# One constant filling product behind each of the first four left-half products of the second layer's tail

## The chip, the cores and the metric

The kernel runs on one core of a Trainium2 chip. The metric is the device time of one execution in microseconds (us); lower is better. Before the change three runs took 203.88, 204.24 and 204.27 us, a median of 204.24 us.

## The reference

Attention over 32 pooled memory slots feeds a soft mixture of eight experts. Per batch and head (8 batches, 8 heads, 576 tokens, 64 wide), and then over all 4608 tokens of 512 numbers:

```
a = softmax(phi, over tokens)                    # 576 x 32
k_m, v_m = a.T @ k, a.T @ v
attn = softmax(q @ k_m.T / 8) @ v_m              # x: 4608 x 512 over all heads
logits = x @ moe_phi                             # 4608 x 32 slots
slot_input = softmax(logits, over tokens).T @ x  # 32 x 512, four slots an expert
h = relu(slot_input[e] @ w1[e])                  # 512 -> 1024, 8 experts
slot_out[e] = h @ w2[e]                          # 1024 -> 512
out = softmax(logits, over slots) @ slot_out     # 4608 x 512
```

All inputs and the output are float32. The weights w1 and w2 are 16.8 MB each and the output is 9.4 MB.

## The kernel before

The work is a list of operations, each with an engine, an estimated cost, the tiles it reads and writes, and a priority. `Plan.order` simulates the engines with these costs and fixes one order per engine; the chip then runs each engine's list in that order, with waits on semaphores. All transfers to and from memory are issued by SyncE (SP) on one hardware queue.

The attention of four pairs of batches takes the first 140 us or so. While it ends, the expert weights stream in. The first layer (`expert_in`, L1383) makes h for two groups of four experts. The second layer (`expert_out`, with `mult`, L1432) sums h @ w2 over 16 pieces of w2, one half of the 512 columns into one accumulator each: the left half (d=0) into `kvbank[:, 0]`, the right half (d=1) into `scbank`. Each piece and half is four matmuls of 128 rows by 32 columns, side by side in the array, over 256 moving columns.

The last NT=5 of the 16 pieces are the tail. `tail_out` loads them by halves of 512 KB: first the five left halves, then the five right halves. `tail_mult(0, n)` adds the five left products as their data lands. Then `slot_sums(0)` copies the left accumulator to `cS` (DVE, L1347), sums its four parts with one product with `rep` (PE, L1355), and splits the result into a high and a low part, `sr` (ACT, L1362; DVE, L1367). Two `direct` products (PE, L1571) give the first output tiles from `cS` itself, and `out_mult` (PE, L1587) gives all others from `sr` and the slot weights `cT`. The table `RIGHT` puts the five right-half products `tail_mult(1, m)` between the first left-half output tiles; behind the last of them `slot_sums(1)` does the same for the right columns. Every output tile is copied out of PSUM by ACT (L1563) or DVE (L1564) in turn, over four PSUM banks, and stored by SP (L1600): six stores of 128 KB, ten of 384 KB, then 768, 1536 and 2304 KB.

`fill(n, pri, r)` puts n products of the constant `ones` (128x128) with itself, 256 moving columns wide, into a part of PSUM that nothing reads (`kvbank[:, 1, 256:512]`, PE, L520). Until now the calls give it priorities of `FILL` and above, which the planner places where PE would otherwise wait. With `pri=None` the operation gets the next priority of its phase, like any other.

Of the kernel before, what the change touches and what calls it, by code (L numbers as in the profile page):

```python
# [20 lines left out]
class Plan:  # L21
# [24 lines left out]
    def add(self, eng, cost, fn, r=(), w=(), also=(), pri=None, dma=0.0, slack=0.0, after=()):  # L46
        cost, ni = cost if isinstance(cost, tuple) else (cost, 4)
        i = len(self.ops)
        deps = set()
        tiles = {}  # L50
        for x in r:
            for key in x:
                tiles[key[0]] = None
                if key in self.last_w:
                    deps.add(self.last_w[key])
        for x in w:
            for key in x:
                tiles[key[0]] = None
                if key in self.last_w:
                    deps.add(self.last_w[key])  # L60
                deps.update(self.reads.get(key, ()))
        for x in w:
            for key in x:
                self.last_w[key] = i
                self.reads[key] = []
        for x in r:
            for key in x:
                self.reads.setdefault(key, []).append(i)
        deps.discard(i)
        deps.update(after)  # L70
        tiles = [t for t in tiles if t.pool is not None]
        for t in tiles:
            t.users += 1
        need = tiles + [t for t in also if t not in tiles]
        if pri is None:
            pri = self.phase[0]
            self.phase[0] += self.phase[1]
        self.ops.append((eng, cost, fn, deps, pri, dma, tiles, need, slack, ni))
        return i
# [191 lines left out]
def kernel(  # L271
# [244 lines left out]
    def fill(n, pri, r=()):  # L516
        for _ in range(n):
            add(
                PE, WC,
                lambda: nc.tensor.matmul(  # L520
                    warm.ap, ones, ones.unsqueeze(1).to_broadcast([P, 2, P]),
                    start=True, stop=True,
                ),
                r=[ones_b, *r], w=[warm], pri=pri,
            )
# [799 lines left out]
    NT, NA = 5, 6  # L1325
# [11 lines left out]
    pacc = [b_kv.tile(), b_s2.tile()]  # L1337
# [87 lines left out]
    def mult(dst, e, i, t, d):  # L1425
        u = 2 * e + i
        wide = t.ap.rearrange("p (j t d) -> p j t d", j=2, t=2)
        for k in range(2):
            for j in range(2):

                x = 2 * k + j
                nc.tensor.matmul(  # L1432
                    dst[NS * x: NS * x + NS, :HD],
                    hT()[:, 4 * k + 2 * i + j, NS * e: NS * e + NS],
                    wide[:, j, k, d * HD: d * HD + HD],
                    start=(u == 0),
                    stop=(u == 2 * E - 1),
                    tile_position=(0, NS * x),
                )
# [29 lines left out]
    def tail_mult(d, n, after=()):  # L1469
        e, i, t = tails[n]  # L1470
        return add(
            PE, (0.45, 16), lambda: mult(pacc[d].ap[:, 0], e, i, t, d),
            r=[hTb.part(e // EG), t.part(d)], w=[pacc[d]], after=after,
        )
# [75 lines left out]
    tail_out()  # L1550
    for n in range(NT):
        tail_mult(0, n)
    for bp in range(1, NBP):
        plan.at(SLOT_AT[bp - 1])
        slots(bp)
# [131 lines left out]
```

## Time and profile before

| | |
|---|---|
| median of three runs | 204.24 us (203.88 to 204.27) |
| the profiled execution, its own time | 204.05 us |
| its span, first to last instruction | 202.3 us |
| PE busy | 169.4 us (84%) |
| DVE, POOL, ACT busy | 141.2 (70%), 95.7 (47%), 74.5 us (37%) |
| moved by DMA | 76.47 MB, mean 378 GB/s |
| mean granted TensorE clock | 0.946 of full speed |

The span is what the rows below are measured in; 1.75 us of the execution lie around it. A granted clock of 1.00 is 2.4 GHz and one of 0.50 is 1.2 GHz. A matmul of the program on float32 data shows as two records in the trace (x8 for the four matmuls of one `mult`).

### The profile page before, as it was taken

What the parts mean: (1) busy time and instruction counts of PE and PEld (TensorE: products, weight loads), DVE (VectorE), ACT (ScalarE), POOL (GpSimd) and SP (SyncE); (2) the same over time, 40 slices, a digit from 0 to 9 for tenths busy, and PEclk for the clock granted to TensorE, in tenths of its full rate; (3) what the DMA queues carried; (4) which work ended last, traced back from release to release, by engine and by line L of the source; (5) the groups of instructions that cost most, each with busy time, mean ns of one, the idle gap of its engine ahead of it and who ended that gap; (6) DMA issues with size and microseconds to landing.
All of it is one profiled execution on the core that took longest, in us unless ns stands there. A gap on an engine that the chain in (4) does not pass through costs nothing.

```text
span 202.3 us, 6086 instructions
## 1 busy us (share of the span) xinstructions
PE 169.4 (84%) x2607; PEld 109.0 (54%) x2607; DVE 141.2 (70%) x267; ACT 74.5 (37%) x191; POOL 95.7 (47%) x92
## 2 busy tenths in 40 slices
PE   7999638978599899797999789899999967999900
PEld 6777534645457387464675347565655624457500
DVE  6822641898986899999899996478999601458810
ACT  2022414555431755607463252110238301246600
POOL 7199204789891894889954275000036930000000
PEclk9999999999859999999999999999999995899975
DMA  6999999999999999999999999999999999589996
GB/s 201 366 392 394 381 387 385 386 388 379 402 381 391 386 383 395 387 395 398 421 399 399 421 421 423 416 423 420 416 418 416 352 348 334 202 287 322 402 416 292
DMA packets 31914, 76.47 MB, mean 378 GB/s; under 512 B 1936, under 2 KB 15760, under 8 KB 28176
## 3 DMA queue, kind: packets, MB, share of 16 engines
q1 hardware_dynamic: 31888, 76.09, 99.6%
q8 instruction: 20, 0.33, 0.7%
q14 instruction: 6, 0.05, 0.1%
HBM read 66.65 MB, written 9.44 MB: 376 GB/s over the span
## 4 chain that ended last, share of the span: by engine, by line
PE 43%; DMA 17%; DVE 12%; POOL 11%; SPq 6%; issue 4%; ACT 2%; DVEq 0%; POOLq 0%
DMA arena<-in_v_dram 9%; PE bank L1383 7%; PE bank L1587 6%; SPq L502 6%; PE scbank L813 5%; DMA arena<-in_moe_w_dram 5%; PE kvbank L704 5%; DMA arena<-in_phi_dram 4%; PE bank L882 4%; POOL arena L871 3%; POOL arena L669 3%; POOL arena L648 3%; PE bank L1010 2%; POOL arena L848 2%; DVE arena L606 2%
## 5 line engine op out<-in xcount | busy, mean ns | idle before, releaser
L648 POOL TENSOR_TENSOR arena<-arena 128x1152 f32<-128x1152 f32 x8 | 21.0, 2634 | 19.2 <-ACT arena L641 16.5
L591 DVE STREAM_TRANSPOSE arena<-top 128x1152 f32<-128x1152 f32 x16 | 21.6, 1354 | 8.2 <-DMA top<-in_q_dram 8.2
L704 PE MATMUL kvbank<-arena 64*32 64x128 f32 x1152 | 21.2, 279 | 6.6 <-ACT arena L657 2.5
L520 PE MATMUL kvbank<-ones 128*128 128x256 f32 x82 | 24.2, 434 | 2.4 <-ACT arena L728 1.3
L669 POOL TENSOR_TENSOR arena<-arena 128x128 f32<-128x128 f32 (+2 forms) x32 | 23.4, 731 | 3.2 <-ACT arena L657 1.3
L813 PE MATMUL scbank<-arena 64*64 64x288 f32 x256 | 22.9, 433 | 2.3 <-DVE arena L827 2.3
L1525 POOL TENSOR_TENSOR cT<-cS,cT 32x640 fp32r<-32x640 f32 (+1 forms) x8 | 11.4, 1420 | 26.2 <-ACT cT L1520 25.7
L871 POOL TENSOR_TENSOR arena<-arena,ssm 128x576 f32<-128x576 f32 x16 | 18.3, 1154 | 9.7 <-DVE ssm L867 7.9
L704 PEld LDWEIGHTS kvbank<-arena 64*32 64x32 f32 x1152 | 16.5, 107 | 11.3 <-issue 4.8
L848 POOL TENSOR_TENSOR arena<-arena,smx 128x576 f32<-128x576 f32 x16 | 18.4, 1154 | 6.5 <-DVE smx L843 6.5
L606 DVE TENSOR_REDUCE arena<-arena 128x128 f32<-128x1152 f32 x8 | 17.1, 2146 | 6.0 <-DMA arena<-in_phi_dram 5.9
L882 PE MATMUL bank<-arena 128*128 128x288 f32 x64 | 18.7, 425 | 1.3 <-DVE arena L874 0.8
L520 PEld LDWEIGHTS kvbank<-ones 128*128 128x128 f32 x82 | 16.3, 214 | 6.3 <-ACT arena L728 1.7
L1564 DVE COPY arena<-bank 128x256 f32<-128x256 f32 (+1 forms) x30 | 14.4, 510 | 6.4 <-PE bank L1587 5.0
L1587 PE MATMUL bank<-sr,cT 64*128 64x256 f32 (+1 forms) x100 | 15.2, 363 | 0.5 <-ACT arena L1563 0.2
L827 DVE STREAM_TRANSPOSE arena<-scbank 128x576 f32<-128x576 f32 x16 | 12.3, 766 | 4.4 <-PE scbank L813 4.3
L813 PEld LDWEIGHTS scbank<-arena 64*64 64x64 f32 x256 | 9.6, 137 | 9.9 <-DVE arena L827 3.7
L882 PEld LDWEIGHTS bank<-arena 128*128 128x128 f32 x64 | 11.2, 189 | 6.4 <-issue 1.7
L853 ACT ACTIVATE arena<-arena 128x576 f32<-128x576 f32 x16 | 10.9, 684 | 9.8 <-POOL arena L848 9.7
L1563 ACT COPY arena<-bank 128x256 f32<-128x256 f32 (+1 forms) x24 | 10.4, 445 | 9.8 <-PE bank L1587 8.4
L1587 PEld LDWEIGHTS bank<-sr,cT 64*128 64x128 f32 x100 | 10.1, 191 | 6.9 <-DVE arena L1564 4.1
L1383 PE MATMUL bank<-arena,SIM 128*32 128x256 f32 x224 | 13.2, 390 | 0.2 <-DVE SIM L1264 0.2
(135 smaller groups left out, 265.0 us busy)
## 6 DMA issues: line engine op xcount, KB each, us to landing
arena<-in_moe_w_dram SPq DMA_DIRECT2D x25, 1024.0 KB, 13.3
top<-in_q_dram SPq DMA_DIRECT2D x8, 1152.0 KB, 13.1
arena<-in_k_dram SPq DMA_DIRECT2D x8, 1152.0 KB, 10.1
arena<-in_v_dram SPq DMA_DIRECT2D x8, 1152.0 KB, 12.5
arena<-in_moe_w_dram SPq DMA_DIRECT2D x10, 512.0 KB, 9.2
arena<-in_phi_dram SPq DMA_DIRECT2D x8, 576.0 KB, 7.5
out_dram<-arena SPq DMA_DIRECT2D x10, 384.0 KB, 3.9
out_dram<-arena SPq DMA_DIRECT2D x1, 2304.0 KB, 7.9
```

Source lines behind the costliest of these rows:

```text
L520: lambda: nc.tensor.matmul(warm.ap, ones, ones.unsqueeze(1).to_broadcast([P, 2, P]), start=True, stop=True,),
L591: lambda: nc.vector.transpose(qT.ap.rearrange("p (i u y) -> p u i y", i=2, y=Y), qt.ap[:, h * QT_SZ: h * QT_SZ + QT_SZ].rearrange("p (u i ...
L606: lambda: nc.vector.tensor_reduce(mx.ap[:, c0:c1], ph().rearrange("p c j m -> p c m j"), axis=AX.X, op=ALU.max),
L648: lambda: nc.gpsimd.tensor_tensor(ph(), ph(), mb.ap[:, c0:c1].unsqueeze(2).to_broadcast([P, c1 - c0, J, M]), op=ALU.subtract,),
L669: plus = lambda o, x, y: nc.gpsimd.tensor_tensor(o, x, y, op=ALU.add)
L704: nc.tensor.matmul(acc.ap[M * c: M * c + M, a, : 2 * D], ph()[h0: h0 + HALF, c, j, :], kv()[h0: h0 + HALF, :, c, j * D: j * D + D], start= ...
L813: nc.tensor.matmul(scb.ap[HALF * g: HALF * g + HALF, a, :JY], pair[g].kd.ap[h0: h0 + HALF, i, c].rearrange("p r m -> p (r m)"), pair[g].qT ...
L848: lambda: nc.gpsimd.tensor_tensor(exv(), exv(), bc(mx), op=ALU.subtract),
L871: lambda: nc.gpsimd.tensor_tensor(exv(), exv(), bc(sm), op=ALU.mult),
L882: nc.tensor.matmul(lp.ap[:, :JY], vpb.ap[:, h, :], aT.ap[:, a * JY: (a + 1) * JY], start=(h == 0), stop=(h == H - 1),)
L1383: nc.tensor.matmul(hb.ap[NS * j: NS * j + NS, :256], SIM.ap[:, 2 * i + c, NS * e: NS * e + NS], wv[:, c, 512 * (j // 2): 512 * (j // 2) + ...
L1587: nc.tensor.matmul(po.ap[:, : x.stop - x.start], cT[bp].ap[y: y + HALF, j // 2 * P: j // 2 * P + P], sr.ap[y: y + HALF, t, x], start=(t == 0),
```

## The change

Behind each of the first four left-half products of the tail, one filling product is put on the list, as a reader of the left accumulator, so that the planner places it after that product and before the next one.

```
     for n in range(NT):
         tail_mult(0, n)
+        if n < NT - 1:
+            fill(1, None, [pacc[0]])
     for bp in range(1, NBP):
```

On PE, before, the right product of the piece ahead of the tail and then the five left products of the tail, up to the sum of `slot_sums(0)`. `DMAHW` names the transfer a product waits for:

```order
L1432 MATMUL scbank<-arena 32x256 x4
L1432 MATMUL kvbank<-arena 32x256 [waits DMAHW4_49]
L1432 MATMUL kvbank<-arena 32x256 x3
L1432 MATMUL kvbank<-arena 32x256 [waits DMAHW5_49]
L1432 MATMUL kvbank<-arena 32x256 x3
L1432 MATMUL kvbank<-arena 32x256 [waits DMAHW6_49]
L1432 MATMUL kvbank<-arena 32x256 x3
L1432 MATMUL kvbank<-arena 32x256 [waits DMAHW7_49]
L1432 MATMUL kvbank<-arena 32x256 x3
L1432 MATMUL kvbank<-arena 32x256 [waits DMAHW0_49]
L1432 MATMUL kvbank<-arena 32x256 x3
L1355 MATMUL bank_65<-cS,rep 128x256 [waits DVE_49]
```

And now, on PE, from the end of the first of these left products to the end of the fifth:

```order
L520 MATMUL kvbank<-ones 128x256
L1432 MATMUL kvbank<-arena 32x256 [waits DMAHW5_49]
L1432 MATMUL kvbank<-arena 32x256 x3
L520 MATMUL kvbank<-ones 128x256
L1432 MATMUL kvbank<-arena 32x256 [waits DMAHW6_49]
L1432 MATMUL kvbank<-arena 32x256 x3
L520 MATMUL kvbank<-ones 128x256
L1432 MATMUL kvbank<-arena 32x256 [waits DMAHW7_49]
L1432 MATMUL kvbank<-arena 32x256 x3
L520 MATMUL kvbank<-ones 128x256
L1432 MATMUL kvbank<-arena 32x256 [waits DMAHW0_49]
L1432 MATMUL kvbank<-arena 32x256 x3
```

Four rows of L520 are new, none of them with a wait; every other row of PE stands where it stood, with the wait it had, and the lists of DVE, ACT, POOL and SP are the same row for row.

## Rows read from the trace of the kernel before

**Rows 1.** The page: span, and the granted clock in 40 slices.
```profile
span 202.3 us, 6086 instructions
...
PEclk9999999999859999999999999999999995899975
```

**Rows 2.** PE in order of time, tail's left products: start, us, [idle before <-releaser].
```profile
162.59 0.61 PE L1432 MATMUL kvbank<-arena 128*32 128x256 f32 x8
163.37 0.64 PE L1432 MATMUL kvbank<-arena 128*32 128x256 f32 x8 [0.17 <-DMA arena<-in_moe_w_dram]
...
166.29 0.64 PE L1432 MATMUL kvbank<-arena 128*32 128x256 f32 x8 [0.83 <-DMA arena<-in_moe_w_dram]
```

**Rows 3.** Busy time by stretch: us, PE, PEld, DVE, ACT, POOL, PEclk, DMA share, GB/s.
```profile
50.00:54.00 4.00, 2.55 (x58) 1.45 (x56) 3.96 (x7) 1.07 (x3) 3.40 (x6) 1.00 1.05 399
84.00:88.00 4.00, 2.76 (x106) 1.97 (x113) 4.00 (x5) 1.27 (x2) 2.65 (x3) 1.00 1.05 384
...
163.00:167.00 4.00, 2.12 (x28) 0.47 (x24) 0.00 (x0) 0.00 (x0) 0.72 (x1) 1.00 1.10 349
...
166.95:168.90 1.95, 1.08 (x8) 0.20 (x8) 0.00 (x0) 0.00 (x0) 0.00 (x0) 0.50 1.10 348
168.90:173.75 4.85, 4.31 (x18) 2.50 (x20) 1.27 (x3) 0.75 (x2) 0.00 (x0) 0.50 0.83 273
173.75:178.40 4.65, 4.43 (x53) 2.44 (x52) 2.46 (x7) 1.44 (x5) 0.00 (x0) 1.00 0.60 199
178.40:183.00 4.60, 4.54 (x35) 3.03 (x34) 3.11 (x8) 3.10 (x9) 0.00 (x0) 1.00 0.97 326
183.00:193.00 10.00, 9.32 (x55) 5.90 (x53) 8.40 (x17) 6.21 (x13) 0.00 (x0) 1.00 1.01 367
```

**Rows 4.** The chain of waits that ended last: start, us, what.
```profile
167.81 1.12 PE kvbank L1432 x8
...
168.96 0.44 DVE cS L1347
...
169.44 1.22 PE bank L1355 x2
170.66 1.71 PE bank L1571 x4
172.36 1.01 PE scbank L1432 x8
173.38 0.89 PE bank L1587 x8
174.26 0.57 PE scbank L1432 x8
...
177.79 0.67 PE bank L1587 x8
178.46 0.61 PE scbank L1432 x8
...
179.53 0.70 PE kvbank L1355 x2
180.22 0.86 PE bank L1571 x4
```

**Rows 5.** PE in order of time: filling products elsewhere, one and two of them.
```profile
19.79 0.59 PE L520 MATMUL kvbank<-ones 128*128 128x256 f32 x2
21.72 1.13 PE L520 MATMUL kvbank<-ones 128*128 128x256 f32 x4 [1.34 <-ACT arena L728]
```

**Rows 6.** The last two loads, by line: ns on SP, first and last start.
```profile
L502 SPq DMA_DIRECT2D arena<-in_moe_w_dram x2: 1390/1404/1417, 165.0 to 166.4; - x2
...
DMA to landing us min/median/max: 8.4/8.5/8.5
```

**Rows 7.** The last store, by line.
```profile
L1600 SPq DMA_DIRECT2D out_dram<-arena x1: 333/333/333, 193.4 to 193.4; - x1
...
DMA to landing us min/median/max: 7.9/7.9/7.9
```

More of the change, by code (lines that the diff above doesn't have):

```diff
@@ L1552 @@
         tail_mult(0, n)
+        if n < NT - 1:
+            fill(1, None, [pacc[0]])
     for bp in range(1, NBP):
```

## The prediction

> **What bounds the kernel now.** I read the page first, for where the TensorE clock is not full. It is below 9 tenths in two places ahead of the last 10 us: slices 11 and 12, near 55 us, and slices 34 and 35, near 170 us [rows 1]. The change sits just ahead of the second. Then I read PE in order of time there, to see what it does before the fall. Up to 162.6 us PE is dense. From 163.37 us on it takes one left product of 0.64 us and then waits up to 0.83 us for the next half piece of w2, which lands every 1.45 us or so [rows 2]. In the 4 us from 163 to 167 it is busy for 2.12 us [rows 3]. Behind that the granted clock is 0.50, that is 1.2 GHz, for 166.95 to 173.75 us, and full again from 173.75 on [rows 3].
>
> The chain of waits is read next, to see whether the slow stretch is on the path that sets the end. It is: from the landing of the last left half at 167.8 us the chain runs through PE without a gap beyond the 0.5 us of the DVE copy: the last left product, the sum of slot_sums(0), the two direct products, the first right product, four output products [rows 4]. No DMA wait stands in it after 167.8 us. Last come the stretches with the DMA share, for what is behind PE: the share is 0.83 in 168.9 to 173.75, 0.60 in 173.75 to 178.4, 0.97 in 178.4 to 183, and 1.01 in 183 to 193 [rows 3]. So the kernel's end is PE's chain until about 183 us, and then a full store queue that was filled by it: the last store is issued at 193.4 us and needs 7.9 us to land, to 201.3 of a span of 202.3 [rows 1, 7].
>
> **The change part by part.** Nothing is removed or moved. Added are four products on PE, without a wait of their own, and no other engine gets an instruction.
>
> *The cost of the four.* One filling product shows 0.59 us from start to end, two in a row 1.13 us, so 0.54 to 0.59 us each at full clock [rows 5]. The first stands behind the left product that ends at 163.2 us, where the wait was only 0.17 us [rows 2], so it makes the second left product up to 0.4 us late; the others stand in waits of about 0.8 us (0.83 in the row shown) and leave 0.2 us or more. The second left product then ends near 164.4 us, its filling product near 165.0, some 0.1 to 0.2 us behind the landing for the third; that is made good in the next wait. The fourth filling product starts at 166.9 and ends before 167.5 us, ahead of the landing at 167.8. What hides them is the wait for DMA, so they cost 0. Without that cover, the most that the last could cost the path is its whole 0.59 us. I take 0, because the row of the last gap has 0.83 us of room.
>
> *What they may give.* With them PE is busy in 163 to 167 us for about 2.12 + 4 x 0.54, which is 4.3 and so more than the stretch has: it is nearly dense, with holes of 0.2 to 0.4 us. In 84 to 88 us, where PE was busy for 2.76 of 4 us, the clock stayed at 1.00; in 50 to 54 us, with 2.55 of 4, the clock was full and then fell (the page's slices 11 and 12) [rows 1, 3]. The stretch with the filling products looks like the first of these and denser. Behind it stand the last left product and the wait of 0.5 us for the DVE copy, and then a dense PE. So I forecast that the clock stays full through 174 us.
>
> *The price of the slow clock, along the chain* [rows 4]. Each step is set against the same kind of step at full clock:
> - last left product 1.12 us, against 0.61 at 178.46: 0.51
> - sum of slot_sums(0) 1.22, against 0.70 at 179.53: 0.52
> - the two direct products 1.71, against 0.86 at 180.22: 0.85
> - first right product 1.01, against 0.57 at 174.26: 0.44
> - the first four output products 0.89, against 0.67 at 177.79: 0.22
>
> Together 2.54 us. The DVE copy of 0.44 us stays as it is.
>
> *What is late next.* The right halves: the last of them is issued at 166.4 and lands 8.4 us later, at 174.8 [rows 6]. PE takes it at 178.46 now, and 2.54 us earlier would be 175.9, still 1.1 us behind the landing. The five loads follow each other by 1.4 us on SP [rows 6], so the first lands at about 174.8 - 4 x 1.4 = 169.2 us, and PE would take it at about 170.5. So no wait for DMA comes in their place. The copies out of PSUM stand to PE as they do at full clock from 177.8 on, where the chain goes through PE.
>
> *The store queue.* Stores now begin up to 2.5 us earlier, while right halves are still landing, and from 183 us on the queue is full. What the end can gain is thus bounded by the idle time of the DMA engines that earlier stores can use. That is 0.17 x 4.85 = 0.8 us in 168.9 to 173.75, 0.40 x 4.65 = 1.9 us in 173.75 to 178.4, and 0.03 x 4.6 = 0.1 us in 178.4 to 183 [rows 3], 2.8 us in all. If all of it can be used, the whole 2.54 us reach the end. If only what lies behind the last right half can, it is 1.9 + 0.1 = 2.0 us. I take 2.25 us, since part of the first 0.8 us falls to DMA engines that have finished their share of the loads and are free for a store.
>
> *The sum.* The profiled execution took 204.05 us: 204.05 + 0 - 2.25 = 201.8. The median of the three runs is 0.19 us above that execution, so 202.0 us is the forecast.
>
> **The rivals.**
>
> *The clock falls all the same, at the same place.* For it: PE still waits before each half piece that lands between 164 and 168 us, and the filling products do not touch the 0.5 us wait for the DVE copy. Against it: the stretch becomes denser than 84 to 88 us was. The time would be 204.05 + 0 to 0.6 (the last filling product at half speed would end at about 166.9 + 1.2 = 168.1, behind the landing at 167.8), so 204.2 to 204.8 as a median. The Trainium skill (TensorE: Matmul & The Clock Gate, HAM oscillation — how this bites in real kernels) speaks on this side: it blames idle gaps that each outlast the monitor's window, and by it waits of under a microsecond do no harm and filling them does no good, 204.2 us. The trace of this case does not agree: the clock fell here behind waits such as the 0.83 us shown [rows 2].
>
> *The clock falls one step later.* The mechanism: the filling products hold the clock through 167 us, and the wait from 167.4 to 167.8, together with the one for the DVE copy up to 169, lets it fall at about 170 instead. Then half speed covers only dense work, and as the slow stretch lasts 6.8 us now [rows 3], it costs 3.4 us of the chain instead of 2.54: 204.05 + 0.86 + 0.19 = 205.1 us, slower than before. It decides from the point where the clock falls behind about 169.5 us. For it: the fall came in both places of the trace a little after a thin stretch. Against it: only about 1 us of waits remains between 167 and 169 us, beside 1.2 us of work. The Trainium skill (TensorE: Matmul & The Clock Gate, What's actually happening) says that the monitor's window runs freely and does not start with the kernel, so a transition can come at another place in another run. The three times before lie within 0.39 us, so no run here shows that yet.
>
> *The store queue keeps most of it.* The clock holds, PE's chain is 2.5 us earlier, but the stores that come during the last loads wait behind them on the engines that are latest, and a full queue carries that to the end. Two thirds lost would leave 0.9 us: 203.3 us. For it: the share is already 0.97 from 178.4 us. Against it: 1.9 us of idle time lie between, in 173.75 to 178.4.
>
> **How the numbers follow.** The forecast has a chance of 0.73; its own range is from 2.54 us with no loss, 201.7, and somewhat less for the spread of the runs, 201.3, to a gain of 1.2 us, 203.0. The store queue that keeps most has 0.09, up to 203.7. The same fall has 0.10, and the later fall 0.08. A measurement of this kernel tells 0.2%, that is 0.4 us, from no change. Faster takes the first two, 0.82; of the same fall 0.08 come out within 0.2% and 0.02 slower; with the later fall, slower is 0.10. The range of 201.3 to 203.7 holds 0.82 of the chance and leaves out the two falls.
>
> **What would show it.** Right: the granted clock is 1.00 throughout 163 to 178 us; the last left product takes 0.6 us in the chain, the direct products 0.9; PE takes the first right product near 169.8 to 170.5 and the last near 176 without a wait for DMA; the DMA share between 171 and 176 is above what it was; the last store is issued near 190.9 and lands near 199. Wrong: a clock of 0.50 anywhere in 166 to 176 us; a left product that starts late behind a filling product at 167.8 us; PE waiting for a right half; or the last store issued early and landing more than 9 us later, which would be the queue.

## The result and the profile after

The changed kernel took 201.56, 201.62, 201.68 and 202.12 us, a median of 201.65 us, beside 203.70 to 204.27 us (median 204.06, four runs) of the kernel before: a ratio of 0.9888, 95% interval 0.9866 to 0.9911. The gain is 2.41 us; 2.25 us were forecast, and a median of 202.0 us. On three chips, in the experiments below, the kernel before spread over 201.1 to 205.2 us; on the one of them where the changed kernel ran beside it, the gain at the median was 1.5 us. Ratios leave out every run more than 1.5% above the fastest of its kernel, in the experiments 16 of the 75 runs of the kernel before; medians and counts leave out none. How much of the spread the clock explains is the main thing the experiments found.

The page of the changed kernel, its profiled execution of 202.12 us:

```profile
span 200.3 us, 6102 instructions
...
PEclk9999995799988999999999999999999999999995
```

The low digits near 170 us of [rows 1] are gone. The earlier low digits moved: 5 and 7 between 30 and 40 us and 8 and 8 between 55 and 65 us, where the kernel before had 8 and 5 between 51 and 61 us. No instruction there was changed.

PE in order of time at the tail, to be read against [rows 2]:

```profile
163.57 0.61 PE L1432 MATMUL kvbank<-arena 128*32 128x256 f32 x8
164.12 0.70 PE L520 MATMUL kvbank<-ones 128*128 128x256 f32 x2
164.75 0.64 PE L1432 MATMUL kvbank<-arena 128*32 128x256 f32 x8
...
167.71 0.70 PE L520 MATMUL kvbank<-ones 128*128 128x256 f32 x2
168.34 0.64 PE L1432 MATMUL kvbank<-arena 128*32 128x256 f32 x8
```

PE reached the first left product at 163.57 us, 1 us later than before (162.59), after a dense stretch; that is ahead of anything changed. From there left products and filling products stand back to back, 1.2 us a pair, with no wait for a landing at all.

Busy time by stretch, columns as in [rows 3]:

```profile
163.00:167.00 4.00, 4.00 (x46) 1.65 (x38) 0.00 (x0) 0.00 (x0) 1.56 (x2) 1.00 1.10 351
166.95:168.90 1.95, 1.95 (x20) 0.61 (x18) 0.00 (x0) 0.00 (x0) 0.00 (x0) 1.00 1.10 348
168.90:173.75 4.85, 4.30 (x44) 2.36 (x40) 2.41 (x6) 1.39 (x4) 0.00 (x0) 1.00 1.03 338
173.75:178.40 4.65, 4.37 (x46) 2.71 (x43) 2.41 (x7) 2.11 (x7) 0.00 (x0) 1.00 0.88 298
```

The granted clock (third from the right) is 1.00 where it was 0.50, and the DMA share of 173.75 to 178.4 us rose from 0.60 to 0.88: the stores fill the idle time that the sum had counted on.

The chain of waits, start, us, what, against [rows 4]:

```profile
167.78 0.63 PE kvbank L520 x2
168.41 0.61 PE kvbank L1432 x8
...
169.05 0.43 DVE cS L1347
...
169.53 0.70 PE bank L1355 x2
170.23 0.86 PE bank L1573 x4
171.09 0.57 PE scbank L1432 x8
171.66 0.68 PE bank L1589 x8
172.34 0.57 PE scbank L1432 x8
```

Each step has the length that the sum had set for full clock (0.61, 0.70, 0.86, 0.57, and 0.68 where 0.67 was set). New is the first row: a filling product in the chain. The last left half was issued at 158.1 us and landed 9.8 us later:

```profile
L502 SPq DMA_DIRECT2D arena<-in_moe_w_dram x1: 1894/1894/1894, 158.1 to 158.1; - x1
...
DMA to landing us min/median/max: 9.8/9.8/9.8
```

So at 167.9 us the data was there, and PE took it at 168.4, behind the filling product. The last store, by line, against [rows 7]:

```profile
L1602 SPq DMA_DIRECT2D out_dram<-arena x1: 332/332/332, 191.5 to 191.5; - x1
...
DMA to landing us min/median/max: 7.9/7.9/7.9
```

It is issued 1.9 us earlier and needs the same 7.9 us to land.

### The profile page after: what moved, and what is told of

It reads as the page before. It is cut to its first block, busy times and chain, and to the rows that moved or that the text cites. A ratio compares the mean times of both kernels' runs of the same rounds, so it can differ in the third digit from the quotient of the medians.

```text
span 200.3 us, 6102 instructions
## 1 busy us (share of the span) xinstructions
PE 171.0 (85%) x2615; PEld 109.9 (55%) x2615; DVE 141.2 (70%) x267; ACT 74.5 (37%) x191; POOL 95.6 (48%) x92
## 4 chain that ended last, share of the span: by engine, by line
PE 49%; DVE 14%; POOL 12%; DMA 8%; issue 4%; SPq 4%; ACT 3%; DVEq 0%; POOLq 0%
DMA arena<-in_v_dram 8%; PE bank L1383 7%; PE bank L1589 6%; PE scbank L813 6%; PE kvbank L704 5%; SPq L502 4%; PE bank L882 4%; PE kvbank L1432 4%; PE scbank L1432 4%; POOL arena L848 3%; POOL arena L871 3%; POOL arena L669 3%; POOL arena L648 3%; PE bank L1010 2%; PE kvbank L520 2%
## 5 line engine op out<-in xcount | busy, mean ns | idle before, releaser
L520 PE MATMUL kvbank<-ones 128*128 128x256 f32 x90 | 27.2, 437 | 2.4 <-ACT arena L728 1.3
L704 PE MATMUL kvbank<-arena 64*32 64x128 f32 x1152 | 21.7, 283 | 6.5 <-issue 2.7
L813 PE MATMUL scbank<-arena 64*64 64x288 f32 x256 | 23.8, 448 | 2.2 <-DVE arena L827 2.2
L520 PEld LDWEIGHTS kvbank<-ones 128*128 128x128 f32 x90 | 17.6, 213 | 8.0 <-issue 2.7
```

Source lines behind the costliest of these rows:

```text
L520: lambda: nc.tensor.matmul(warm.ap, ones, ones.unsqueeze(1).to_broadcast([P, 2, P]), start=True, stop=True,),
L704: nc.tensor.matmul(acc.ap[M * c: M * c + M, a, : 2 * D], ph()[h0: h0 + HALF, c, j, :], kv()[h0: h0 + HALF, :, c, j * D: j * D + D], start= ...
L813: nc.tensor.matmul(scb.ap[HALF * g: HALF * g + HALF, a, :JY], pair[g].kd.ap[h0: h0 + HALF, i, c].rearrange("p r m -> p (r m)"), pair[g].qT ...
```

## The experiments

Two theories. The clock theory: the gain is the slow stretch that no longer falls on the chain behind the last left product. The rival: it comes from something else that the four products change, or from ahead of the tail. Each experiment edits the lines of the change.

**Two moving columns instead of 256 (e1 and e11).**

```
-            fill(1, None, [pacc[0]])
+            add(PE, 0.1, lambda: nc.tensor.matmul(warm.ap[:, :2], ones, ones[:, :2],
+                start=True, stop=True), r=[ones_b, pacc[0]], w=[warm])
```

> The four filling products keep their places and their number of instructions, but stream 2 moving columns each instead of 256, so PE's waits for the half pieces stay nearly as long as before the change. If the gain comes from PE being busy there (the clock theory), the granted clock falls to 0.50 near 167 us again, the direct products take about 1.7 us in the chain, and the time is that of the kernel before, 203.7 to 204.4 us. If the gain comes from anything else that four more instructions change (where PE's instructions are fetched, the order), the time is that of the changed kernel, 201.5 to 202.1 us.

> A second trace of the filling products with 2 moving columns. In the first, PE came to the tail late, hardly waited, and the clock was full, 201.8 us; its other runs spread from 200.97 to 204.53 us. If filling products must be wide to hold the clock, this one shows, in 7 of 12 cases by the spread, a stretch at 0.50 behind 166 us and 202.4 us or more. If their mere number holds it, a full clock.

Measured: e1 took 200.97 to 204.53 us in 12 runs, median 202.78, beside 203.26 (201.29 to 205.0, 29 runs) of the kernel before. Neither expectation: it spreads as the kernel before does. Its trace, at 201.8 us, had a full clock; PE came late there and hardly waited. e11, at 203.38 us, shows the fall with the same instructions. PE in order of time in e11, its last two narrow products and the left products beside them:

```profile
165.02 0.38 PE L1556 MATMUL kvbank<-ones 128*128 128x2 f32 x2
165.87 0.90 PE L1432 MATMUL kvbank<-arena 128*32 128x256 f32 x8 [0.46 <-DMA arena<-in_moe_w_dram]
166.70 0.59 PE L1556 MATMUL kvbank<-ones 128*128 128x2 f32 x2
167.37 1.08 PE L1432 MATMUL kvbank<-arena 128*32 128x256 f32 x8
```

In the middle of the second row the products get longer: the granted clock is 0.50 from 166.2 to 172.9 us. So four more instructions in these places did not hold the clock there, with waits of up to 0.47 us left between them. The products of 128 columns below did, with waits of up to 0.41 us. Whether it is the columns or the somewhat shorter waits beside them is not told apart.

**Half the columns (e2, and e7 beside the changed kernel, e6).**

```
-            fill(1, None, [pacc[0]])
+            add(PE, 0.3, lambda: nc.tensor.matmul(warm.ap[:, :128], ones, ones[:, :128],
+                start=True, stop=True), r=[ones_b, pacc[0]], w=[warm])
```

> The four filling products stream 128 moving columns instead of 256, about 0.4 us each in the chain instead of the 0.63 us that the changed kernel's trace shows. In the changed kernel's profiled execution PE came to the tail 1 us later than in the one before, and left products and filling products stood back to back, so that the last left product started 0.43 us behind its landing. If the clock holds with half the columns, that is given back: last left product at its landing, time 201.2 to 201.7 us. If half is too little to hold the clock, it falls near 167 us and the time is 203.7 to 204.4 us.

> The changed kernel with more runs, on one chip with the next one. If its filling products hold the clock in every run, all runs lie between 201.2 and 202.3 us, where the kernel before has 201.3 to 205. If they hold it in some runs only, some lie at 203 to 205 us.

> The half-width filling products beside the full-width ones on one chip. If full-width ones cost something on the path (0.43 us in the trace of the changed kernel, where PE came late and never waited for a landing), this one is 0.2 to 0.5 us faster, 200.9 to 201.5 us in all runs. If they cost nothing, both are the same within 0.1 us.

Measured: e2 200.99 to 201.44 us (6 runs, median 201.25). On one chip, 12 runs each: the changed kernel 201.57 us (200.99 to 202.97), half width 201.57 us (201.26 to 202.2), the kernel before 203.02 us (201.06 to 205.12, 29 runs). The ratios to before are 0.9973 (0.9935 to 1.0011) and 0.9955 (0.9922 to 0.9989): by them the changed kernel is not clear of no change on this chip, and half width is. The counts further below separate both from the kernel before. Half width holds the clock too, and at the median it gains nothing over full width: of the two outcomes expected of e7 it was the second.

Two of the changed kernel's 12 runs, 202.71 and 202.97 us, lie above the 202.3 us that the expectation had set. They left no trace. Their mean granted clocks over the whole run are the lowest of the twelve, 0.945 and 0.944 where the others have 0.960 or more, so the clock was low for longer in them; but e1 and e12 have 0.946 and 0.945 in traces with a full clock at the tail, so where it was low stays open. PE in order of time in e7 shows the room that half width leaves:

```profile
166.79 0.49 PE L1556 MATMUL kvbank<-ones 128*128 128x128 f32 x2
167.65 0.64 PE L1432 MATMUL kvbank<-arena 128*32 128x256 f32 x8 [0.37 <-DMA arena<-in_moe_w_dram]
```

and in e6, with full width and PE on time, two rows of the same place:

```profile
164.90 0.64 PE L1432 MATMUL kvbank<-arena 128*32 128x256 f32 x8 [0.15 <-DMA arena<-in_moe_w_dram]
...
167.68 0.64 PE L1432 MATMUL kvbank<-arena 128*32 128x256 f32 x8
```

**Filling products in two of the four places (e3, e4).**

```
-        if n < NT - 1:
+        if n < 2:               # e3; in e4: if 2 <= n < NT - 1:
```

> Filling products behind the first two left products only. PE is dense to about 165 us and waits as before up to 169 us. By the rival of the later fall the clock holds through 167 and falls near 170 us, where half speed covers dense work alone: 204.5 to 205.3 us, slower than the kernel before. If the clock holds altogether, 201.2 to 201.9 us. If it falls near 167 as before, 204 us.

> Filling products behind the third and fourth left products only. If the clock theory holds, what counts is that PE does not get thin for long ahead of the dense stretch: two of four waits filled. Clock held: no filling product stands where PE comes late, so the last left product starts nearer its landing, 201.2 to 201.8 us. Clock not held, with a fall near 167 us: 204 us, or a bit more, since the filling products then run at half speed.

Measured: behind the first two, 201.10 to 204.26 us (12 runs, median 201.60), 8 of them below 202.3 us. Behind the last two, 201.12 to 201.76 us in 11 runs and 203.32 us in the profiled one (median 201.59). Both traces have a full clock at the tail. The 203.32 us of e4 come from elsewhere: its last left product starts at 169.56 us, 0.9 to 2.3 us later than in the other traces, because half pieces landed late. In its chain PE comes late before that, the load of the last left half starts at 158.94 us, 0.6 us later than in e6, and takes 10.6 us to land where e6 has 9.3; why the landing took longer is open. Nothing near the 204.5 to 205.3 us of the rival appears at e3's median. Four of e3's runs lie above 202.3 us, one of e4's and two of the changed kernel's 16; only e4's left a trace, so it is not shown that the first two alone hold the clock less reliably.

**Two filling products in each place (e8).**

```
-            fill(1, None, [pacc[0]])
+            fill(2, None, [pacc[0]])
```

> Two full-width filling products behind each of the first four left products instead of one. A left product and two of them take 0.57 + 2 x 0.63 = 1.83 us back to back, where the half pieces land every 1.5 us; four such steps from 162.7 to 163.6 us end at 170.0 to 170.9, so the last left product starts 2 to 3 us behind its landing, and with a clock that holds the time is 203.2 to 204.6 us. If the end were set by the store queue or by something else behind PE, less than half of that would reach it: 201.6 to 202.6 us.

Measured: 202.56 to 203.71 us (12 runs, median 202.83), 1.26 us above the changed kernel on the same chip. That is between the two outcomes. Two in a row take 1.06 us, not 2 x 0.63, so the last left product is less late than worked out: it starts at 168.69 us, 1.0 us later than in e6. The planner also put some right products in pairs in this kernel, and behind the last left product its trace takes 0.3 us more, so the size is not the filling products' alone. The direction stands: what delays the last left product reaches the end.

**A fifth one, behind the last left product, at half width (e12).**

```
-        if n < NT - 1:
+        if n < NT:              # with the half-width product
```

> Half-width filling products behind all five left products, so one more in the wait of 0.55 us for the DVE copy, where about 0.49 us of it fit. If that wait still lets the clock fall in some runs, this takes away what is left of the spread: all runs 201.0 to 201.8 us. If the fifth delays the sum of slot_sums(0), up to 0.3 us more than with four, 201.3 to 202.1 us.

Measured: 201.84 to 203.02 us (12 runs, median 201.95), the second outcome, with four runs above its 202.1 us. The chain of e12 shows why:

```profile
168.19 0.64 PE kvbank L1432 x8
168.83 0.43 PE kvbank L1556 x2
...
169.28 0.44 DVE cS L1347
```

The DVE copy is released by the filling product and not by the left product ahead of it, though it needs nothing of the filling product: 0.43 us are on the path. Both touch the one PSUM tile `kvbank`, in different parts; that this makes the wait is likely, but not shown.

**The kernel before, three more traces (e5, e9, e10).** No edit.

> The kernel before once more, for its trace. In the runs beside the first four experiments it took 201.29 to 205.0 us, 7 of 29 runs below 202.1 and the other 22 above 202.8, so it seems to have two or more outcomes. Clock theory: a run above 202.8 us shows a stretch at 0.50 between 163 and 178 us, and a run below 202.1 us shows none there. Rival (the spread comes from the earlier falls, near 30 to 60 us, which delay the whole): a slow run shows a full clock at the tail and left products that start a microsecond or more later than 167.8 us.

> One more trace of the kernel before. So far its slow stretch at the tail lay at 166.95 to 173.8 us (204.05 us) and at 169.0 to 172.4 us (202.59 us). Clock theory: the time follows from how much of 167 to 178 us the trace shows at 0.50. None: 201.0 to 202.1 us, the changed kernel's time without a filling product. About 3.4 us: 202.5 to 203.3. About 6.8 us: 203.7 to 205.1. Rival (the spread comes from ahead of the tail): no such relation, and the last left product starts later in a slow run.

> A further trace of the kernel before, with the same three outcomes: none of 167 to 178 us at 0.50 and 201.0 to 202.1 us; about 3.4 us and 202.5 to 203.3; about 6.8 us and 203.7 to 205.1.

Measured: 202.59, 202.65 and 203.76 us. e5 lies between the two outcomes of its expectation, and its stretch at 0.50, 169.0 to 172.3 us, is there as the clock theory has it. e9 and e10 then lie where the length of their slow stretch had put them. The chain of e9, where the clock fell a little later than in [rows 4]:

```profile
167.34 0.68 PE kvbank L1432 x8
...
168.52 1.22 PE bank L1355 x2
169.75 1.71 PE bank L1571 x4
171.45 0.66 PE scbank L1432 x8
172.11 0.68 PE bank L1587 x8
```

The last left product is at full clock, two steps are slow, and the first right product is nearly at full clock again. Busy time by stretch for e9 and then e10, 166 to 175 us, to read the clock:

```profile
166.00:175.00 9.00, 7.57 (x64) 3.89 (x56) 2.59 (x7) 1.57 (x5) 0.00 (x0) 0.81 0.93 303
```

```profile
166.00:175.00 9.00, 7.60 (x52) 3.75 (x55) 2.03 (x5) 1.42 (x4) 0.00 (x0) 0.62 0.89 287
```

A mean of 0.81 over 9 us is 0.19 x 9 / 0.5 = 3.4 us at half speed, one of 0.62 is 6.8 us.

All traces in one table. The last column is the span less the start of the last left product, so what lies before that (landings, a late PE, filling products in its way) is taken out:

| kernel | time, us | clock, 166 to 175 us | last left product starts | span | from there to the end |
|---|---|---|---|---|---|
| before | 204.05 | 0.62 | 167.81 | 202.3 | 34.5 |
| before (e10) | 203.76 | 0.62 | 167.38 | 202.0 | 34.6 |
| two columns (e11) | 203.38 | 0.62 | 167.37 | 201.6 | 34.2 |
| before (e9) | 202.65 | 0.81 | 167.34 | 200.9 | 33.6 |
| before (e5) | 202.59 | 0.81 | 167.25 | 200.8 | 33.6 |
| two columns (e1) | 201.80 | 1.00 | 168.00 | 200.0 | 32.0 |
| first two (e3) | 201.90 | 1.00 | 168.11 | 200.1 | 32.0 |
| last two (e4) | 203.32 | 1.00 | 169.56 | 201.5 | 31.9 |
| changed | 202.12 | 1.00 | 168.34 | 200.3 | 32.0 |
| changed (e6) | 201.46 | 1.00 | 167.68 | 199.7 | 32.0 |
| half width (e2) | 200.99 | 1.00 | 167.22 | 199.2 | 32.0 |
| half width (e7) | 201.53 | 1.00 | 167.65 | 199.8 | 32.1 |
| five, half width (e12) | 202.45 | 1.00 | 168.19 | 200.7 | 32.5 |
| two each (e8) | 202.73 | 1.00 | 168.69 | 201.0 | 32.3 |

With a full clock the rest takes 31.9 to 32.1 us (e12 has its 0.43 us more, e8 its pairs of right products), whether the filling products are wide, narrow or missing in two places. With 6.8 us at half speed it takes 34.2 to 34.6, with 3.4 us 33.6; in e11, with the 34.2, the fall began 1.2 us ahead of the last left product, so less of it lies behind. This settles the price of the slow clock on the chain behind the last left product: 2.2 to 2.6 us and 1.6 us. What a fall costs ahead of that product the table does not show.

By counts of all runs below 202.3, from there to 203.4, and above: the kernel before 18, 22 and 35 of 75 beside the experiments; two columns 5, 4 and 4 of 13; the changed kernel 14, 2 and 0 of 16; half width 18, 0 and 0 of 18. That the runs of the kernel before in the lowest class had a full clock at the tail was not seen: none of its four traces fell into it. The trace of e1 is the nearest. The mean granted clock over the whole run, which each run has, points the same way (0.958, 0.952 and 0.943 on average in the three classes of the kernel before), but the classes overlap in it, and it does not say where the clock was low.

## Why the prediction was right, point by point

**The clock holds.** Right. It is full through 163 to 178 us in both traces of the changed kernel and both of half width. The step rested on PE being nearly dense there; it came out fully dense (4.00 of 4 us), partly because PE was late in that execution. In e6, with PE on time, it was busy for 3.61 of 4 us, with the same full clock.

**The price, 2.54 us.** Right for the traced execution: 34.5 - 32.0 = 2.5 us in the table, and each of the five steps shrank to the length set for it. That it is the whole gain at the median too was in part luck. All four runs before lay above 203.4 us, where 35 of 75 lie beside the experiments; from a trace like e9's the same reckoning would have given 1.6 us.

**Filling products cost 0.** Not in the profiled execution. PE came to the tail 1 us late and the cover, the wait for the next landing, was gone, so a sign that the prediction had named for being wrong did show, a left product that starts late behind a filling product: the last left product started at 168.41 us in the chain, 0.60 us later than before, 0.43 of it behind a filling product and 0.17 because the half landed later. The prediction had named the whole 0.59 us as the cost without cover. In e6, where PE was on time, there is a wait of 0.15 us left beside them, the last left product starts 0.04 us behind the landing of its half in the chain, and half width is no faster at the median, so usually the cost is about nothing.

**The store queue keeps 0.3 us.** Wrong, it kept nothing: the last store is issued 1.9 us earlier and lands 1.9 us earlier. The bound from the idle time of all DMA engines, 2.8 us, was the end to take, since the share between 168.9 and 178.4 us rose to 1.03 and 0.88.

The sum of the profiled execution is thus 204.05 - 2.54 + 0.43 + 0.17 = 202.11, measured 202.12 us. That the forecast of 201.8 for it was near is in part luck: what it missed, 0.43 and 0.17 us on one side and 0.29 on the other, is small and opposite. PE took the first right product at 171.1 us, later than the 169.8 to 170.5 us forecast, and without a wait for its landing, as forecast.

**The rivals.** The same fall at the same place did not come in any trace with filling products of 128 or 256 columns. The store queue's rival fell with the table: an equal 32.0 us behind starts that differ by 2.3 us. The later fall is the one that was half right, though of the kernel before: there the clock does fall at another place in another run, at 168.2 and 169.0 us in e9 and e5 against 167.0 us. But then it stayed low for 3.4 us instead of 6.8, so it costs less and not more: 1.6 us instead of the 3.4 worked out. The Trainium skill (TensorE: Matmul & The Clock Gate, What's actually happening) says that a transition may come at another place in another run; the four traces of the kernel before agree, with falls from 166.9 to 169.0 us. The four times before, within 0.6 us of each other, had hidden that. They had also hidden that the times of this program spread by 4 us; the prediction had taken 0.4 us as enough to tell a change from none.

What stays open: the changed kernel's two runs near 202.8 us, and why the last landing in e4 took longer. For PE's late arrival at the tail the traces have a likely cause, the early falls of the clock. Busy time from 28 to 65 us in the changed kernel's first trace and then in e6, with the granted clock third from the right:

```profile
28.00:65.00 37.00, 29.90 (x587) 18.45 (x569) 27.07 (x37) 15.22 (x38) 25.41 (x23) 0.86 1.04 379
```

```profile
28.00:65.00 37.00, 30.43 (x651) 19.23 (x634) 28.86 (x40) 15.28 (x39) 25.43 (x23) 0.91 1.05 385
```

A mean of 0.86 over 37 us is 10 us at half speed, one of 0.91 is 6.7 us. By finer stretches nine of the fourteen traces have 3.4 or 6.8 us there, and PE starts the first transposes of h (L1410) at 144.9 to 145.8 us; three have 10.2 us (the changed kernel's first, e4, e10) and start them at 146.1 to 147.8 us; two have 13.7 us (e1, e12) and start them at 147.2 and 147.3 us. Every trace with 10 us or more at half speed there came later than every one with less; no experiment changed that part, so it is not shown as the cause.

## What to carry to other kernels

Where a stage waits for transfers in short steps and dense work on the path follows, read the granted clock behind the stage, not the waits in it: here waits of under 1 us cost 2.5 us later on. A constant product of 128 or 256 columns in each such wait kept the clock full in all six traces that have one in each, and was nearly free where it was shorter than the wait; let no other engine's wait include it (0.43 us in e12). Take several traces before pricing such a fall, and compare from a fixed event, such as the start of the last product fed by a load, to the end.

## What was not expected of the hardware

In four traces of the kernel before, the slow stretch at the tail began at 166.9, 167.0, 168.2 or 169.0 us and lasted 6.8 us in the first two and 3.4 us in the others, and its time spread from 201.1 to 205.2 us with nothing changed. With narrow products (2 moving columns, 0.38 us each in the trace) the profile shows PE busy for 3.04 of 4 us in 163 to 167 us of e11, and yet the clock fell within that stretch:

```profile
163.00:167.00 4.00, 3.04 (x30) 1.37 (x30) 0.00 (x0) 0.00 (x0) 0.00 (x0) 0.89 1.05 347
```

With half-width products e7 shows 3.07 us busy in the same stretch, and a full clock:

```profile
163.00:167.00 4.00, 3.07 (x31) 1.28 (x30) 0.00 (x0) 0.00 (x0) 0.22 (x1) 1.00 0.97 326
```

So PE's busy time in the profile does not tell these two apart.
